# Strassen's scheme for the MLP's first product on half of the tiles, in a two-layer linear-attention and MLP kernel

## The chip, the cores and the metric

The kernel runs on one core of a Trainium2 chip. The metric is the device time of the whole program in microseconds. Of the core's engines, TensorE (PE) does matrix products into PSUM; VectorE (DVE), ScalarE (ACT) and GpSimd (POOL) do the work on elements; SyncE (SP) issues nearly all DMA transfers. Each engine works through its instructions in program order and waits on semaphores of the others.

## The reference

```python
def _A_ref(x, wqkv, wo):                 # D = 448, H = 16, Dh = 28
    qkv = (x @ wqkv) ...                 # q, k, v by heads
    phi = lambda t: jnp.where(t > 0, t + 1, jnp.exp(t)) + 1e-6
    pq, pk = phi(q), phi(k)
    kv = einsum("bhsd,bhse->bhde", pk, v); z = einsum("bhsd->bhd", pk)
    o = einsum("bhqd,bhde->bhqe", pq, kv) / (einsum("bhqd,bhd->bhq", pq, z)[..., None] + 1e-6)
    return o (heads joined) @ wo
def _B_ref(x, w1, b1, w2, b2):           # F = 1792
    return gelu(x @ w1 + b1) @ w2 + b2
x = A_x                                  # 1 x 2048 x 448
x = x + _A_ref(_layernorm(x), A_wqkv, A_wo)
x = x + _B_ref(_layernorm(x), B_w1, B_b1, B_w2, B_b2)
...                                      # the same two lines once more, same weights
```

All arrays are float32.

## The kernel before

The 2048 rows of x are 16 tiles of 128 rows, in four blocks of four tiles. F is 14 chunks of 128. Each operand of a product is split into a high part (rounded to the type float32r) and a low part (the rest, float32r too), and a product takes three matmuls: high by high, high by low, low by high. The inner size 448 is three pieces of 128 rows and one of 64; in that last piece the weights' high and low parts lie under each other in one tile of 128 rows, so that it takes two matmuls. A product over 448 is eleven matmuls.

A layer has four stages. The first (`phase1`) goes over the 16 tiles: normalize, transpose, project k and q, and gather the sums `G` over all tiles. The second (the list `ORDER`) makes the matrices that give the attention output and treats block 0. The third is the MLP, block by block: for chunk i, `mlp1(l, b, i + 1)` makes the next chunk's hp (128 features by 512 rows, eleven matmuls of 512 columns), ACT takes the gelu into g and casts it to gh, DVE makes gl; then `mlp2(l, b, i)` adds the chunk's product with w2 to four PSUM tiles y (four row tiles, three matmuls of 448 columns each). Between the two, `behind` issues the work for the following blocks by the lists PLAN_0, PLAN_1 and PLAN: `z` multiplies on POOL, `p` scales the stored q by its denominators and transposes it on DVE, `sq`/`lq` store it to DRAM and load it back spread over partitions (4 DMAs), `q` splits it, `o` is the attention product (11 matmuls of 448 columns) and the residual add with its statistics, `n` normalizes and transposes, `sx`/`lx` store and load again, `x` splits the result into the block's XH and XL. Beside block 3 the next layer's first five tiles are prepared and wk, wq are split again.

The high and low parts of w1 (`w1h`, `w1l`, `w1x`) and of w2 (`w2h`, `w2l`) are made once, in layer 0, by `background`, piece by piece, and stay in SBUF for both layers. The order on every engine is the program's order; no planner changes it.

`mlp1` takes its moving rows from a block as one run of 512 columns:

```python
def moving(self, x, c):
    return x[:, c * 512:(c + 1) * 512]
```

In the prediction, y names the products of mlp2, hp those of mlp1, gh and gl the split of the gelu's result.

Of the kernel before, what the change touches and what calls it, by code (L numbers as in the profile page):

```python
# [22 lines left out]
def linear_attn_mlp_kernel(  # L23
# [22 lines left out]
    NG = D // G  # L46
    TL = D - 64
# [115 lines left out]
    one = t512("e", 3, "one")[:, :128]  # L163
# [9 lines left out]
    none = consts.tile([128, 6], F32, name="none")  # L173
    none, rs0, sums = none[:, :1], none[:, 1:2], none[:, 2:]
    waste = t512("xn", 2, "waste")
# [3 lines left out]
    mhalf = consts.tile([128, 2], F32, name="mhalf")  # L179
    mhalf, eps = mhalf[:, :1], mhalf[:, 1:]  # L180
    pool.memset(mhalf, -0.5)
    pool.memset(eps, 1e-5)
    tiny = consts.tile([128, 1], F32, name="tiny")
    pool.memset(tiny, 1e-6)
    zc = consts.tile([128, 1], F32, name="zc")
# [11 lines left out]
    w1h = wts.tile([128, 3, F], F32R, name="w1h")  # L197
    w1l = wts.tile([128, 3, F], F32R, name="w1l")
    w1x = wts.tile([128, F], F32R, name="w1x")
    w2h = wts.tile([128, NF, D], F32R, name="w2h")  # L200
    w2l = wts.tile([128, NF, D], F32R, name="w2l")

# [22 lines left out]
    def ln_norm(stats, name, centre=OP.subtract):  # L225
        xs, mv, rs = stats
        xn = t512("xn", 2, name)
        dve.tensor_scalar(xn[:, :D], xs, mv[:, 0:1], rs, op0=centre, op1=OP.mult)
        return xn

    class Block:
        def __init__(self, key):
            at = APART if key[0] == "a" else 0
            self.rows = key[0] == "m"
            self.hi = work.tile([128, 2048], F32R, name="XH", tag="XH", bufs=2)
            self.lo = work.tile([128, 2112], F32R, name="XL", tag="XL", bufs=2)[:, at:at + 2048]

        def pieces(self, t):  # L240

            if self.rows:
                return tuple(x.rearrange("p (c t n) -> p t c n", c=4, t=4)[:, t] for x in (self.hi, self.lo))
            s = slice(t * 512, (t + 1) * 512)
            return self.hi[:, s], self.lo[:, s]

        def moving(self, x, c):

            return x[:, c * 512:(c + 1) * 512]

        def still(self, x, t, c):

            return x[:, (t * 4 + c) * 128:(t * 4 + c + 1) * 128]
# [63 lines left out]
    def spread(key, h, queues=(sp,)):  # L317
        d = stored.pop((key, h))
        r = spreads[key, h] = half("sp") if d.shape[1] == 1024 else half_square("sp", h)
# [17 lines left out]
    def turn_one(x, key, j):  # L337
# [4 lines left out]
                      x[:, TL:D].rearrange("p (m n) -> p m n", n=32)[:, None].to_broadcast([128, 2, 2, 32]))  # L342

# [19 lines left out]
    def proj(name, key, j, o=None, cs=range(4), at=(3, 6, 9, 11)):  # L363
# [3 lines left out]
        if len(cs) == 4:  # L367
            w = [wkq[name, c] for c in range(3)]
            his = [(b.still(b.hi, j, c), p) for c in range(3) for p in w[c]] + [(b.still(b.hi, j, 3), wkq[name, 3])]
            los = [(b.still(b.lo, j, c), w[c][0]) for c in range(3)] + [(b.still(b.lo, j, 3), wkq[name, 3])]  # L370
# [3 lines left out]
        for c in cs:  # L374
            if c < 3:
                hi, lo = wkq[name, c]
                pe.matmul(o, b.still(b.hi, j, c), hi, start=(c == 0), stop=False)
                pe.matmul(o, b.still(b.hi, j, c), lo, start=False, stop=False)
                pe.matmul(o, b.still(b.lo, j, c), hi, start=False, stop=False)
            else:  # L380
                pe.matmul(o, b.still(b.hi, j, 3), wkq[name, 3], start=False, stop=False)
                pe.matmul(o, b.still(b.lo, j, 3), wkq[name, 3], start=False, stop=True)
        return o

    def phi(o, name, into=None, tag="e"):

        e = t512(tag, 3 if tag == "e" else 2, name)[:, :D]
# [7 lines left out]
    def bg_pieces():  # L395
        n = 0
        both = []

        def stage():
            nonlocal n  # L400
            n += 1
            if n <= LATE:
                k = (n - 1) // 2
                if k % 2 == 0 or k > 5:
# [858 lines left out]
```

## Time and profile before

| | |
|---|---|
| time, median of 3 runs (lowest, highest) | 864.05 us (863.78, 864.33) |
| the profiled execution's own time | 864.72 us |
| its span, from first to last instruction | 863.0 us |
| PE, DVE, ACT, POOL busy | 99%, 57%, 41%, 25% of the span |
| matmuls | 4155 |
| DMA | 97.89 MB in 68681 packets |

In the rows below, a group has the line, the engine, the operation, what it writes and reads, its shape and count, then busy time, mean duration in ns, and the engine's idle time before it with what ended it. A row of one line's durations has minimum, median and maximum in ns. A row of a wait has who waited for whom, the microseconds in total, the times, and the longest. A row of the timeline has the start, the duration, and the instruction; a row of the chain has the start, the length, and the work. A matmul's duration there is longer than the distance to the next matmul's start, since matmuls are pipelined.

### The profile page before, as it was taken

The page shows a single profiled execution, that of the slowest core. Times are in us where ns is not written, and L with a number is a line of the kernel's source. Part 1 is how long each engine was busy: PE and PEld are TensorE (multiplying, and loading weights), DVE is VectorE, ACT ScalarE, POOL GpSimd, SP SyncE. Part 2 cuts the span into 40 slices and gives each one's busy share as a digit, 9 for nine tenths or more (in the row PEclk, how much of TensorE's full clock was granted, in tenths as well). Part 3 has the DMA queues.
Part 4 walks back from the last instruction along what each step waited for, and adds up shares of the span by engine and source line. Part 5 has one row for each costly group of instructions (what it writes and reads, how often), then busy time and mean ns, then how long its engine had stood idle before and what let it go on. Part 6 is the DMA issues. An engine that isn't in the chain of part 4 may idle for free.

```text
span 863.0 us, 11715 instructions
## 1 busy us (share of the span) xinstructions
PE 857.2 (99%) x4155; PEld 768.1 (89%) x4155; DVE 493.0 (57%) x962; ACT 352.8 (41%) x635; POOL 211.6 (25%) x244
## 2 busy tenths in 40 slices
PE   9999999999999999999999999999999999999998
PEld 8999988888888888888899998988888888888887
DVE  7888586559456443236477876764664383533112
ACT  7676655323323322333356565633232233233231
POOL 3576612235013012012222343120310140140000
PEclk9999999999999999999999999999999999999999
DMA  5485647633313402051146442462332423111001
GB/s 171 150 270 180 206 108 217 191 113 121 123 61 123 140 0 98 1 182 49 49 150 188 164 130 96 146 204 81 123 113 78 140 74 111 49 49 43 1 1 43
DMA packets 68681, 97.89 MB, mean 113 GB/s; under 512 B 9488, under 2 KB 62864, under 8 KB 68624
## 3 DMA queue, kind: packets, MB, share of 16 engines
q1 hardware_dynamic: 67872, 96.76, 35.0%
q8 instruction: 32, 0.52, 0.3%
q10 hardware_dynamic: 752, 0.41, 0.2%
q14 instruction: 25, 0.20, 0.1%
HBM read 57.74 MB, written 36.18 MB: 109 GB/s over the span
## 4 chain that ended last, share of the span: by engine, by line
PE 90%; DVE 4%; DMA 3%; issue 1%; ACT 1%; POOL 1%; SPq 0%; DVEq 0%; ACTq 0%; POOLq 0%
PE hp L1011 32%; PE y L1041 10%; PE y L1040 10%; PE y L1042 10%; PE psq L372 5%; PE G L658 5%; PE psk L372 5%; PE op L949 2%; PE op L948 2%; PE op L950 2%; DMA sp<-sq_a 1%; PE op L938 1%; PE op L937 1%; PE op L939 1%; PE kvp L824 1%
## 5 line engine op out<-in xcount | busy, mean ns | idle before, releaser
L1017 DVE TENSOR_TENSOR gl<-g,gh 128x512 fp32r<-128x512 f32 x112 | 83.2, 743 | 293.0 <-ACT gh L1016 293.0
L1013 ACT ACTIVATE g<-hp,b1s 128x512 f32<-128x512 f32 x112 | 77.1, 689 | 400.8 <-PE hp L1011 400.8
L1041 PE MATMUL y<-w2l,gh 128*128 128x448 f32 x447 | 163.6, 366 | 0.0
L1040 PE MATMUL y<-w2h,gh 128*128 128x448 f32 x447 | 162.0, 362 | 0.0
L1042 PE MATMUL y<-w2h,gl 128*128 128x448 f32 x447 | 160.0, 358 | 0.0
L1011 PE MATMUL hp<-XH,w1h 128*128 128x512 f32 x336 | 130.7, 389 | 0.0
L1011 PE MATMUL hp<-XH,w1l 128*128 128x512 f32 x336 | 130.7, 389 | 0.0
L1011 PE MATMUL hp<-XL,w1h 128*128 128x512 f32 x336 | 130.1, 389 | 0.0
L216 POOL TENSOR_TENSOR brs<-bve,mhalf 128x1 f32<-128x1 f32 x55 | 34.2, 622 | 258.5 <-DVE bve L215 250.8
L1040 PEld LDWEIGHTS y<-w2h,gh 128*128 128x128 f32 x447 | 83.7, 187 | 9.4
L1041 PEld LDWEIGHTS y<-w2l,gh 128*128 128x128 f32 x447 | 83.9, 188 | 7.0
L1042 PEld LDWEIGHTS y<-w2h,gl 128*128 128x128 f32 x447 | 84.0, 188 | 5.0
L1011 PEld LDWEIGHTS hp<-XL,w1h 128*128 128x128 f32 x336 | 63.1, 188 | 13.1
L1011 PEld LDWEIGHTS hp<-XH,w1h 128*128 128x128 f32 x336 | 63.0, 187 | 10.7
L1011 PEld LDWEIGHTS hp<-XH,w1l 128*128 128x128 f32 x336 | 63.1, 188 | 9.9
L1016 ACT CAST gh<-g 128x512 fp32r<-128x512 f32 x112 | 69.6, 621 | 3.6
L372 PE MATMUL psk<-wk,XH 128*128 128x448 f32 x210 | 61.8, 364 | 0.0
L372 PE MATMUL psq<-wq,XH 128*128 128x448 f32 x196 | 57.0, 365 | 0.0
L497 POOL TENSOR_TENSOR xnl<-x,xnh 128x384 fp32r<-128x384 f32 x32 | 35.0, 1094 | 73.5 <-ACT xnh L496 60.3
L355 DVE TENSOR_TENSOR XL<-sp,XH 128x512 fp32r<-128x512 f32 x58 | 47.2, 825 | 5.7 <-ACT XH L354 5.7
L883 POOL TENSOR_TENSOR pz<-pq,zb 128x448 f32<-128x448 f32 x24 | 28.2, 1174 | 89.9 <-DVE dn L894 61.8
L658 PE MATMUL G<-kh,xnh 128*128 128x448 f32 x128 | 46.7, 367 | 0.0
(194 smaller groups left out, 1500.2 us busy)
## 6 DMA issues: line engine op xcount, KB each, us to landing
x<-in_A_x_dram SPq DMA_DIRECT2D x32, 224.0 KB, 3.9
pq_d<-eq SPq DMA_DIRECT2D x32, 224.0 KB, 2.5
pq<-pq_d SPq DMA_DIRECT2D x32, 224.0 KB, 3.6
x<-x_d SPq DMA_DIRECT2D x32, 224.0 KB, 3.9
sq_a<-sq SPq DMA_DIRECT2D x13, 512.0 KB, 2.9
sp<-sq_a SPq DMA_DIRECT2D x52, 128.0 KB, 2.9
sq_q<-sq SPq DMA_DIRECT2D x12, 512.0 KB, 2.6
sp<-sq_q SPq DMA_DIRECT2D x48, 128.0 KB, 2.8
```

Source lines behind the costliest of these rows:

```text
L216: pool.tensor_tensor(rs, ve, mhalf, op=OP.pow)
L355: eng.tensor_tensor(lo.rearrange("p c (i n) -> p c i n", n=32), x, f(h), op=OP.subtract)
L372: pe.matmul(o, x, p, start=(i == 0), stop=(i == 10))
L497: pool.tensor_tensor(lo[:, :TL], xn[:, :TL], f(h[:, :TL]), op=OP.subtract)
L658: pe.matmul(acc[c], w, k, start=first and c not in others[0], stop=last and c not in others[1])
L1011: pe.matmul(hp, w, r, start=(k == 0), stop=(k == len(made) - 1))
L1013: act.activation(g, hp, AF.Gelu_apprx_tanh, bias=b1s[:, i:i + 1])
L1016: act.copy(gh, g)
L1017: dve.tensor_sub(gl, g, f(gh))
L1040: pe.matmul(acc[j], gh[:, s], w2h[:, i], start=first, stop=False)
L1041: pe.matmul(acc[j], gh[:, s], w2l[:, i], start=False, stop=False)
L1042: pe.matmul(acc[j], gl[:, s], w2h[:, i], start=False, stop=stop)
```

## The change

Blocks 0 and 1 of a layer keep the products described above (`classic`). Blocks 2 and 3, the last eight tiles, are treated together. Their 1024 rows are split into two halves of 512 columns, the inner size 448 into an upper 256 and a lower 192, and each pair of w1's chunks into its two chunks. On these two by two pieces runs Strassen's scheme (Winograd's form): seven products in place of eight, on sums and differences of the weights' pieces and of the tokens' pieces.

Each pair of chunks comes from DRAM again whenever it is used, for each layer and three times in a layer (blocks 0, 1 and the pairs of blocks 2 and 3), and is split anew into one of two buffers W1: by `chunks` for the classic blocks, by `sevens` for Strassen's pieces. `make(n)` issues one step of such a generator, and the calls of `make` are placed among the other work.

The attention work for blocks 1, 2 and 3 now all lies beside the two classic blocks, in one new list PLAN of 28 steps. The residual rows of these blocks are stored to r_d after the attention add and come back by `back` when they are needed. The token sums S1 to S4 are made in the last steps of PLAN (tokens `s` and `t`), the odd halves on DVE and the even ones on POOL, each then split into high (ACT) and low (DVE). The y products of the last two chunks of block 1 are held back into the first pair.

In a pair, block 2's two chunks go on to mlp2 beside the following products; block 3's gelu results are stored to g_d, and when all seven pairs are done `rest` loads them, splits them, and runs mlp2 for block 3 without other products, with the next layer's first tiles beside it.

The tokens' buffers XH and XL are now one tile each, with every tile's four pieces together, so that a classic product's moving rows are four runs of 128 columns:

```diff
-        def moving(self, x, c):
-            return x[:, c * 512:(c + 1) * 512]
+        def moving(self, k, c):
+            at = self.key[2] * 2048
+            return (XH, XL)[k][:, at:at + 2048].rearrange("p (t n) -> p t n", t=4)[:, :, c * 128:(c + 1) * 128]
...
-    w1h = wts.tile([128, 3, F], F32R, name="w1h")
-    w1l = wts.tile([128, 3, F], F32R, name="w1l")
-    w1x = wts.tile([128, F], F32R, name="w1x")
+    W1 = wts.tile([128, 2, 25 * 128], F32R, name="W1")
...
+    def top(x, hi, lo):
+        act.copy(hi, x)
+        pool.tensor_tensor(lo, x, f(hi), op=OP.subtract)
+    def low(x, w):
+        act.copy(w[:, :512], x)
+        pool.tensor_tensor(w[64:, 256:512], x[64:, 256:], f(w[64:, 256:512]), op=OP.subtract)
+        pool.tensor_tensor(w[:, 512:768], x[:, :256], f(w[:, :256]), op=OP.subtract)
...
+    def sevens(n):
+        came = raw(n)
+        yield
+        ...
+        low(down, w)
+        yield
+        top(t1, u[:, 6:10:2], u[:, 7:10:2])
+        dve.tensor_copy(down[:, 256:], f(w[:, 256:512]))
+        yield
+        pool.tensor_tensor(t1, t3, t1, op=OP.subtract)
+        pool.tensor_tensor(t3, t2, t3, op=OP.subtract)
+        yield
+        pool.tensor_tensor(t2, t2, t1, op=OP.subtract)
+        pool.tensor_tensor(t4, t4, t2, op=OP.subtract)
+        yield
+        act.copy(w[:, 1280:1792], up)
+        sp.dma_start(fold[:64], t4[64:, 1])
+        sp.dma_start(fold[64:], t4[:64, 1])
+        yield
+        dve.tensor_tensor(w[:, 2304:2816], up, f(w[:, 1280:1792]), op=OP.subtract)
+        yield
+        pool.tensor_tensor(t4[:, 1], t4[:, 1], fold, op=OP.add)
+        yield
+        act.copy(w[:, 1792:2304], down)
+        yield
+        dve.tensor_tensor(w[:, 2816:3072], down[:, :256], f(w[:, 1792:2048]), op=OP.subtract)
+        dve.tensor_tensor(u[:, 24], t2[:, 1], f(u[:, 16]), op=OP.subtract)
+        dve.tensor_tensor(u[64:, 17], t4[64:, 1], f(u[64:, 17]), op=OP.subtract)
+        yield
...
+    SUMS = {"S1": ("A21", "A22", OP.add), "S2": ("S1", "A11", OP.subtract),
+            "S3": ("A11", "A21", OP.subtract), "S4": ("A12", "S2", OP.subtract)}
+    def token_sum(l, name, h):
+        eng = (pool, dve)[h]
+        ...
+    def token_piece(l, name, h, eng=dve):
+        x = view(l, name, h)
+        hi, lo = (cols(placed(l, k, name, h)) for k in range(2))
+        act.copy(hi, x)
+        eng.tensor_tensor(lo, x, f(hi), op=OP.subtract)
+    PRODUCTS = {1: ((6, 7, 8, 9), "A11"), 2: ((1, 5, 3), "A12"), 3: ((0, 4, 2), "S4"), 4: ((15, 23, 17), "A22"),
+                5: ((11, 19, 13, 21), "S1"), 6: ((14, 22, 16, 24), "S2"), 7: ((10, 18, 12, 20), "S3")}
...
+    PLAN = (
+        "p10 z11",
+        ...
+        "q13 o12 n11 sx10 p20 z21",
+        ...
+        "q22 o21 n20 p30 z31",
+        "q23 o22 n21 sx20 p31 z32 sq30",
+        ...
+        "n33 lx30 sx31 tA110 b13",
+        "lx31 sS10 tA120",
+        "tS10 sS30 sS20",
+        "tS20 sS40 sS11 tS11 sS31",
+        "tS40 sS21 tS21 sS41",
+        "tA220 tA221 tS41",
     )
...
+    def eight(l, k):                     # one pair of chunks on blocks 2 and 3
+        n = first_pair(l, 2) + k
+        c = Pair(l, k, n)
+        def step():
+            if k < NP - 1:
+                make(n + 1)
+        c.product(1)
+        s1 = c.keep(c.X, "s1")           # ACT copy out of PSUM
+        if k == 0:
+            make(n, 2)
+            beside(l, k)                 # here: the pieces S30, S31
+        step()
+        if k == 0:
+            mlp2(l, 1, NF - 2)
+            c.product(2)
+            mlp2(l, 1, NF - 1)
+        c.product(5)
+        s5 = c.keep(c.Y, "s5")
+        step()
+        if k == 0:
+            dve.tensor_tensor(s1, s1, c.Z, op=OP.add)
+        if k:
+            mlp2(l, 2, 2 * k - 1)
+        c.product(6)
+        s2 = c.keep(c.X, "s2")
+        step()
+        if k == 0:
+            c.high(s1, 0)                # gelu in two halves, cast to gh
+        else:
+            c.product(2)
+            dve.tensor_tensor(s1, s1, c.Z, op=OP.add)
+            c.high(s1, 0)
+            step()
+        c.product(7)
+        dve.tensor_tensor(s5, c.X, s5, op=OP.add)
+        c.low(0)                         # gl
+        c.later(s5, 1)                   # gelu, store to g_d
+        step()
+        c.product(3)
+        dve.tensor_tensor(s2, s2, c.Y, op=OP.add)
+        c.high(s2, 1)
+        step()
+        c.product(4)
+        if k == NP - 1:
+            gb.load(l, 2)
+        c.low(1)
+        c.later(c.X, 0)
+        step()
+        if k < NP - 2:
+            make(n + 2)
+        if k:
+            beside(l, k)                 # wk, wq loads and splits, residuals back
+        step()
+        mlp2(l, 2, 2 * k)
+        step()
...
-        mlp1(l, 0, 0)
-        trans_chunks(tr)
-        for b in range(NB):
-            ...
+        for b in range(2):
+            classic(l, b, tr)
+        for k in range(NP):
+            eight(l, k)
+        if l + 1 < LAYERS:
+            table(AF.Exp)
+        rest(l)
```

Products 1, 6, 7 and 4 add up in one PSUM tile X, products 5 and 3 in Y, product 2 is Z; s1, s5 and s2 are copies of what X and Y hold at their time.

513 lines of the change are left out of this document (330 added, 183 removed), and 8 rows, old and new, of tables (ORDER, STEPS).

## The prediction

> **What bounds the kernel now.** I read the page's busy shares and slices first, then the chain of work that ended last, then TensorE's own waits.
>
> ```profile
> span 863.0 us, 11715 instructions
> PE 857.2 (99%) x4155; PEld 768.1 (89%) x4155; DVE 493.0 (57%) x962; ACT 352.8 (41%) x635; POOL 211.6 (25%) x244
> DVE  7888586559456443236477876764664383533112
> PEclk9999999999999999999999999999999999999999
> PE 90%; DVE 4%; DMA 3%; issue 1%; ACT 1%; POOL 1%; SPq 0%; DVEq 0%; ACTq 0%; POOLq 0%
> PE hp L1011 32%; PE y L1041 10%; PE y L1040 10%; PE y L1042 10%; PE psq L372 5%; PE G L658 5%; PE psk L372 5%; PE op L949 2%; PE op L948 2%; PE op L950 2%; DMA sp<-sq_a 1%; PE op L938 1%; PE op L937 1%; PE op L939 1%; PE kvp L824 1%
> ...
> PE warm L170 <- DVE one L164: 1.1, 1, 1.1
> PE psk L586 <- ACT wk L137: 0.9, 1, 0.9
> PE psk L372 <- DVE XL L355: 0.2, 1, 0.2
> ```
>
> TensorE (PE) is busy for 857.2 of 863.0 us at full clock, and its waits come to 2.2 us, nearly all at the start. Time goes down only by issuing fewer matmuls, and goes up by every new hole in PE. A busy PE need not run at its pitch, so I checked the pitch in the chain's order of time and in one timeline:
>
> ```profile
> 363.80 2.49 PE hp L1011 x11
> 368.70 2.49 PE hp L1011 x11
> ...
> 476.76 2.20 PE psq L372 x11
> ...
> 380.59 0.39 PE L1011 MATMUL hp<-XL,w1x 128*128 128x512 f32 x1
> 380.81 0.36 PE L1040 MATMUL y<-w2h,gh 128*128 128x448 f32 x1
> 381.01 0.69 ACT L1013 ACTIVATE g<-hp,b1s 128x512 f32<-128x512 f32 x1 [3.55 <-PE hp L1011]
> 381.73 0.62 ACT L1016 CAST gh<-g 128x512 fp32r<-128x512 f32 x1
> 382.39 0.70 DVE L1017 TENSOR_TENSOR gl<-g,gh 128x512 fp32r<-128x512 f32 x1 [4.20 <-ACT gh L1016]
> 383.21 0.39 PE L1011 MATMUL hp<-XH,w1h 128*128 128x512 f32 x1
> 383.44 0.39 PE L1011 MATMUL hp<-XH,w1l 128*128 128x512 f32 x1
> ...
> ```
>
> Eleven matmuls of 448 columns take 2.20 us, 0.2002 each. One chunk of the MLP is 368.70 − 363.80 = 4.90 us and holds eleven of 512 and twelve of 448; 4.895 − 12 × 0.2002 = 2.49, so a 512-column matmul costs 0.2265 us of PE. The same rows give the way round: 0.20 us after the next product begins ACT starts on the old one, and gl is there 2.3 us after PE ended hp.
>
> **The product counts.** A pair of chunks on two blocks takes 2 × 2 × 11 = 44 matmuls of 512 columns; Strassen's seven products take 6+5+5+5+6+6+6 = 39 (the list PRODUCTS: four weight pieces give six matmuls, three give five, since the 64 last rows carry high and low part in one piece). Seven pairs, two layers: 14 × 5 = 70 fewer, 70 × 0.2265 = 15.9 us. Nothing else in PE's list changes number. This is the whole gain, and the ceiling: 864.05 − 15.9 = 848.2.
>
> **The two classic blocks.** All attention output work of blocks 1 to 3 now lies beside two blocks instead of three.
>
> ```profile
> 134.00:202.00 68.00, 68.00 (x322) 60.17 (x321) 42.77 (x79) 25.68 (x44) 24.71 (x22) 1.00 0.55 169
> 202.00:264.00 62.00, 62.00 (x295) 55.13 (x295) 34.21 (x69) 17.88 (x29) 9.12 (x9) 1.00 0.33 110
> 264.00:333.00 69.00, 69.00 (x329) 61.32 (x328) 36.95 (x73) 20.98 (x34) 15.60 (x14) 1.00 0.23 78
> ...
> L1017 DVE TENSOR_TENSOR gl<-g,gh 128x512 fp32r<-128x512 f32 x112 | 83.2, 743 | 293.0 <-ACT gh L1016 293.0
> L355 DVE TENSOR_TENSOR XL<-sp,XH 128x512 fp32r<-128x512 f32 x58 | 47.2, 825 | 5.7 <-ACT XH L354 5.7
> L431 POOL TENSOR_TENSOR w2l<-stg,w2h 128x448 fp32r<-128x448 f32 x14 | 16.5, 1181 | 36.2 <-ACT w2h L430 36.2
> ...
> L1045 DVE TENSOR_TENSOR x<-y,x x32: 610/614/625, 213.6 to 858.8; 128x448 f32<-128x448 f32 x32
> ```
>
> The columns after the stretch are its length, then PE, weight loads, DVE, ACT, POOL. DVE: 42.8 + 34.2 + 37.0 = 113.9 us. Out go 14 gl (10.4), 4 adds of y (2.5) and 8 block pieces (6.6); in come 14 token pieces at 0.825 and four half sums of some 0.75 (14.6): 109 us in 28 × 4.895 + 12 × 2.20 = 163.5 us, 67%. Per tile the parts q, o, n, p come to (113.9 − 42 × 0.743 − 12 × 0.614 − 12 × 0.825) / 12 = 5.5 us; the densest steps hold all four (of four tiles) and a gl, 6.2 us of DVE in 4.9 + 2.2 = 7.1 us of PE; gl has 4.9 − 2.3 = 2.6 us to spare, so I cost this at nothing. The cover is that slack; should backlog pass it, PE waits for gl once per step. POOL gets the w1 splits, four instructions per pair at about 0.84 (between the rows for 64 and 384 columns below): 14 × 3.4 = 47 us on top of 49.4 less some 14 of w2 (12 of the 14 in its row), half its time. ACT gets 1.4 us per pair (two casts of 256, one of 512). SP gets two loads of w1 per pair, twelve stores and loads of r_d, twelve issues each, and is past its work two steps ahead; all of it waits behind spreads whose store must land first, as before. Layer 0 loses its w1 splits in the first phase and has two pairs' splits beside the Q products; PE has no hole there to win (0.2 us). Zero for these.
>
> The moving rows of the classic product now come as four runs of 128 columns. No row shows such a read by PE. Every product of before has one run; I take zero, as the data per column are the same, and price the other end below.
>
> **The pairs in steady order.** A pair is 39 × 0.2265 + 24 × 0.2002 = 13.64 us of PE: product 1 to 1.36, 5 to 2.72, y to 5.12, 6 to 6.48, 2 to 7.61, 7 to 8.97, 3 to 10.1, 4 to 11.24, y to 13.64. Three places wait: product 7 for the copy s2 on ACT (0.20 + 0.62 after 6, product 2 gives 1.13), product 4 for the add into s5 on DVE (0.20 + 0.69, product 3 gives 1.13), and y for gh and gl (s1 at 8.5, two half gelus and cast to 10.0, gl at 10.8 behind s5; needed at 11.24 and 11.6). All hidden by 0.2 to 0.8 us. ACT is packed from 7.8 to 14 and free again for the next s1 at 15.2. The weight chain of the next pair (about 5.7 us of POOL, 2 of ACT, 2 of DVE) has its late link in the two fold transfers.
>
> ```profile
> wq<-Mh SPq DMA_DIRECT2D x2, 56.0 KB, 2.8
> ...
> wq<-Mh SPq DMA_DIRECT2D x2, 28.0 KB, 4.5
> ```
>
> They are issued behind the store of g, near 10.5 to 11.5; landing after 2.8 or 4.5 us, POOL's add, ACT's cast and DVE's three low pieces end at 16 to 17.5, and product 6 of the next pair wants them at 18.8. Zero, with 1.3 us left at the bad end.
>
> **The join, twice.** Here the cover runs out. Call T the end of the last classic product (chunk 13 of block 1). PE has 1.36 (product 1), 2.40 (y, chunk 12), 1.13 (2), 2.40 (y, chunk 13), then 5, 6, 7 with 1.36 each and 3 with 1.13: product 4 is due at T + 12.5. It needs DVE's add into s5. DVE is free from gl of chunk 12, at T − 4.9 + 2.3 = T − 2.6, and has in order nine pieces, four half sums, gl of chunk 13, W1's low parts (one of 512, one of 256, two of 128: 1.65), two copies of 256 (0.5, an estimate under the 0.42 of the row for 256), four adds of y, s1 and s5.
>
> ```profile
> L355 DVE TENSOR_TENSOR XL<-sp,XH x58: 677/684/1640, 46.1 to 783.2; 128x512 fp32r<-128x512 f32 x58
> L1017 DVE TENSOR_TENSOR gl<-g,gh x112: 681/693/1478, 138.1 to 856.0; 128x512 fp32r<-128x512 f32 x112
> L905 DVE SCALAR_TENSOR_TENSOR pq<-pq,rd x32: 615/1181/1374, 105.5 to 708.2; 128x448 f32<-128x448 f32 x32
> 147.08 1.16 POOL L883 TENSOR_TENSOR pz<-pq,zb 128x448 f32<-128x448 f32 x1
> 147.47 1.25 DVE L905 SCALAR_TENSOR_TENSOR pq<-pq,rd 128x448 f32<-128x448 f32 x1
> L292 DVE TENSOR_TENSOR XL<-tp,XH 128x256 fp32r<-128x256 f32 x4 | 1.6, 422 | 0.4 <-ACT XH L290 0.2
> L290 ACT CAST XH<-tp 128x256 fp32r<-128x256 f32 x4 | 1.4, 368 | 0.1
> L978 POOL TENSOR_TENSOR x<-x,b2b 128x448 f32<-128x448 f32 x32 | 41.9, 1329 | 0.0
> L497 POOL TENSOR_TENSOR xnl<-x,xnh 128x384 fp32r<-128x384 f32 x32 | 35.0, 1094 | 73.5 <-ACT xnh L496 60.3 <-PE psk L372 13.1
> L498 POOL TENSOR_TENSOR xnh<-x,xnh 128x64 fp32r<-128x64 f32 x32 | 14.5, 452 | 0.0
> ...
> ```
>
> At the medians (minimum, median, maximum in these rows): 9 × 0.684 + 5 × 0.69 + 1.65 + 0.5 + 4 × 0.614 + 2 × 0.69 = 15.6 us, so T + 13.0: at least 0.6 us late even if DVE never waits. It does wait: the S1 and S2 halves go sum on DVE, cast on ACT, low part on DVE, 0.65 us empty each, 1.3. And it meets POOL, which in the same time has the S4 half (about 1.45) and four weight differences (0.84 each), 4.8 us. DVE operations with two SBUF inputs stretch beside POOL: the row of pq went from 0.615 to 1.25 us under POOL's pz, while the adds from PSUM stay at 610 to 625 ns. Low end: none, 0.6 in all. High end: POOL's 4.8 us fully in DVE's way, 6.7. I take the row nearest: pieces average 0.825 against 0.684, 0.14 each with POOL busy a quarter of these stretches; at four times that share 0.56 each, five such operations, 2.8, a third of it inside the empty 1.3. So 0.6 + 1.3 + 1.9 = 3.8 us a layer, 7.6 in all. It shows first at product 6 (third of W1's low parts on DVE), then at 7 (S3) and at 4.
>
> The Trainium skill has a rule on this, in "SBUF — State Buffer", section "Who interferes with whom": a VectorE operation with two SBUF inputs and a GpSimd operation that reads SBUF exclude each other, and the second blocks until the first ends. The pq row's 1.25 us agrees. By it alone the join costs its high end, which is the second rival.
>
> **After the pairs.** Block 3's second product runs alone, 2.40 us a chunk, against 0.62 + 0.69 of ACT and DVE for its split.
>
> ```profile
> L205 ACT ACT_TABLE_LOAD x4 | 5.1, 1283 | 1.3 <-PEq L1249 1.3
> ...
> 367.00:432.00 65.00, 65.00 (x308) 57.39 (x307) 31.07 (x55) 23.67 (x40) 13.27 (x13) 1.00 0.28 93
> ```
>
> In layer 0 this table load puts the first gh late and DVE's low part ahead of three adds of y: 0.7 us. The next layer's first tiles lay beside block 3 before (the stretch from 367 us, 31.1 us of DVE with 13 gl and the splits of wk and wq in it); without those splits, which move to the pairs, they fit into 14 × 2.40 = 33.6 us with one chunk of slack for gl: zero.
>
> **The sum.** Against the profiled execution's own 864.72 us: − 15.86 + 7.6 + 0.7 = 857.2; the median of the runs lies 0.67 lower: 856.5.
>
> **The rivals.**
> 1. The join is hidden, as DVE gets ahead and POOL is done before it: 0 to 2 us a layer, 848.9 to 852.9. For it: the four POOL differences depend on nothing of PE and may be through early. Against: 15.6 us of DVE in 15.1 of PE.
> 2. The lock is complete: 6.7 a layer and the same 0.7, 862.3 (861 to 864.5). For it: 1181 as the median of pq. Against: gl's median is the undisturbed 693.
> 3. The strided moving rows cost PE. Two layers have 2 × 28 × 11 = 616 such matmuls. From 0.2265 and 0.2002 a matmul's fixed part is 0.0265 for 64 columns, hence 0.2265 − 0.212 = 0.0145; three more starts each, 0.0435 × 616 = 26.8 us: 883, slower. It decides from 8 / 616 = 13 ns a matmul. For it: the two sides of a split are never seen in the trace. Against: nothing in the chain depends on how rows lie.
> 4. The fold chain is late in every pair by over 0.6 us: 14 × 0.6 eats what is left. Against: 1.3 us of slack at the bad end.
>
> **Chances.** Forecast (852.9 to 861): 0.57. Rival 1: 0.16. Rival 2: 0.15, and it lies across the bound, 0.06 of it faster, 0.08 the same, 0.01 slower. Rival 3: 0.07. Rival 4 and unseen holes: 0.05, 0.01 of it the same. Faster by over 0.2% (1.7 us, about what a measurement of this kernel can tell from no change) 0.79, same 0.09, slower 0.12. Range 850 to 863: it leaves out a third of rival 1, rivals 3 and 4 and the end of 2.
>
> **What would show it.** 1162 matmuls of 512 columns in the MLP's first product at 0.2265 pitch; the classic ones at the same pitch (rival 3 otherwise). PE's waits with DVE low parts and s5 as releasers at two places of the span, some 3 to 4 us each, each just behind the second classic block, and none in pairs 1 to 6. DVE pieces near 1.2 us there. If PE waits for gl in the classic blocks, my zero there is wrong; if for W1 in later pairs, the chain's.

## The result, and the profile after

The changed kernel takes 930.15 us (929.2 to 931.75 in four runs) where the kernel before, measured beside it, took 864.19: a ratio of 1.0765, 95% interval 1.0746 to 1.0783. It is 66 us slower than before, and 82 us above the 848.2 that the matmul counts promised. One execution of e1_raw_early (1724.71 us) and one of e8_before_off64 (1070.89 us), far slower than the others of their kernels, are left out of the times below. The first fence is from the page of the kernel after: span, busy time, the granted clock in forty slices, the chain that ended last by engine and by line.

```profile
span 927.9 us, 12697 instructions
PE 878.6 (95%) x4085; PEld 760.6 (82%) x4085; DVE 590.8 (64%) x1094; ACT 444.0 (48%) x869; POOL 390.8 (42%) x460
PEclk9999999998999999999999999999999999999999
PE 49%; DMA 18%; DVE 12%; ACT 6%; SPq 5%; issue 4%; POOL 4%; DVEq 0%; ACTq 0%; POOLq 0%
DMA raw<-in_B_w_dram 8%; PE G L726 8%; PE psk L385 7%; PE psq L385 7%; PE hp L1201 5%; PE y L1233 3%; PE y L1231 3%; PE y L1232 3%; DMA temp<-in_B_w_dram 3%; DMA sq_q<-sq 3%; PE hx L1143 2%; SPq L333 2%; DVE gl L1178 2%; ACT g L1155 2%; DVE pq L975 1%
```

The 70 matmuls are gone (4155 to 4085). But PE carries 49% of the chain instead of 90%, and DMA 18% instead of 3%: its first entry is the load of w1 for the pairs (`raw<-in_B_w_dram`, 8% of the span), with the classic blocks' load (`temp`) and the stores of sq_q behind it. PE's waits, the largest ones (line, what it waited for: us in all, times, longest; hx, hy and hz are a pair's tiles X, Y and Z, op is the attention product, ql and qh the split of its q, W the pieces of w1):

```profile
PE hx L1143 <- ACT s L1147: 20.4, 12, 2.7
PE op L1025 <- DVE ql L368: 4.2, 4, 1.6
PE y L1233 <- DVE gl L1178: 4.2, 4, 1.2
PE hx L1143 <- DVE W L478: 2.6, 2, 1.3
PE hp L1201 <- POOL W L434: 2.3, 4, 1.1
PE hy L1143 <- DVE W L472: 2.1, 2, 1.2
```

The stretches of layer 0 (length, then busy PE, weight loads, DVE, ACT, POOL, the granted clock, DMA share, GB/s): classic blocks, join, six steady pairs, and the rest up to the next layer.

```profile
134.99:306.23 171.24, 166.76 (x754) 142.99 (x752) 115.70 (x214) 64.77 (x119) 80.45 (x86) 0.98 0.62 190
306.23:327.99 21.76, 17.43 (x64) 12.43 (x63) 19.19 (x27) 10.94 (x22) 12.53 (x14) 0.92 0.13 47
327.99:424.47 96.48, 86.39 (x379) 71.62 (x378) 40.06 (x65) 52.51 (x110) 42.71 (x49) 0.98 0.30 93
424.47:470.01 45.54, 41.44 (x193) 35.43 (x192) 29.63 (x55) 17.36 (x32) 16.70 (x18) 1.00 0.70 227
```

From these lengths I take what the matmuls would need at the pitches of before (the pitch is the time from one matmul's start to the next one's): 158.65 us for the classic blocks (28 × 2.4915 + 26 × 2.4024 + 12 × 2.2022), 13.63 for the join, 6 × 13.64 for the pairs and 16 × 2.40 for the rest. What is left is the loss of a stage. The table has it for layer 0 / layer 1, worked out in this way from the trace of each kernel:

| us lost in | classic | join | six pairs | rest | time of the kernel |
|---|---|---|---|---|---|
| after | 12.6 / 11.1 | 8.1 / 8.2 | 14.6 / 15.1 | 7.1 / 1.7 | 930.15 |
| first load early (e1b) | 10.8 / 12.4 | 7.3 / 7.7 | 1.5 / 1.5 | 5.8 / 1.9 | 898.67 |
| no classic loads (e2) | 4.6 / 4.3 | 6.1 / 6.6 | 15.3 / 11.4 | 7.1 / 1.7 | 906.7 |
| split load (e16) | 8.0 / 6.3 | 6.1 / 7.1 | 2.1 / 1.4 | 2.3 / 1.4 | 886.66 |
| split load and four more edits (e17) | 4.1 / 2.7 | 4.6 / 4.6 | 1.5 / 1.4 | 2.7 / 1.3 | 871.66 |

For the kernel after the eight losses sum to 78.5; with some 2 us in the first stages that is 848.2 + 80.5 = 928.7, against 930.15. Every stage lost, those that I had costed at nothing most.

This is how the pairs lose, in the timeline of pair 1 of layer 0 (start, length, and in brackets the idle time before):

```profile
332.20 0.58 SPq L423 DMA_DIRECT2D raw<-in_B_w_dram  x1
339.25 0.62 ACT L432 CAST W<-raw 128x512 fp32r<-128x512 f32 x1 [6.14 <-DMA raw<-in_B_w_dram]
340.55 0.59 ACT L1147 COPY s<-hx 128x512 f32<-128x512 f32 x1
341.19 1.65 PE L1143 MATMUL hx<-S,W 128*128 128x512 f32 x6 [2.73 <-ACT s L1147]
```

SP issues the second part of pair 2's load at 332.20. Within pair 1, ACT comes to the cast that starts pair 2's weight chain, and stands 6.14 us until the load is there. The copy s2 (at 340.55), whose data PE had finished, is behind that cast in ACT's order; product 7 needs s2's bank, and PE stands 2.73 us. The wait is booked to ACT, but a DMA ends last. That the load takes 6.5 us, the same timeline shows; why, the windows behind its issue show in the DMA share:

```profile
332.20:334.00 1.80, 1.80 (x10) 1.53 (x9) 0.92 (x3) 0.90 (x2) 0.00 (x0) 1.00 0.94 240
334.00:336.00 2.00, 2.00 (x11) 1.85 (x10) 0.00 (x0) 0.00 (x0) 0.00 (x0) 1.00 0.38 111
336.00:338.00 2.00, 2.00 (x10) 1.66 (x9) 0.00 (x0) 0.00 (x0) 0.00 (x0) 1.00 0.14 49
338.00:339.00 1.00, 0.47 (x3) 0.03 (x1) 0.00 (x0) 0.00 (x0) 0.00 (x0) 1.00 0.07 26
```

From 336 on the share is 0.14 at 49 GB/s: two of sixteen engines work, 2 / 16 = 0.125, and 128 KB / 49 GB/s is 2.7 us. That is the copy of w1's last 64 rows into both halves of the tile, one transfer with an outermost dimension of 2 (`to_broadcast([2, 64, 256])`). The Trainium skill says just this in "DMA: Bandwidth & Descriptors", section "Rules for kernel authors": a transfer whose outermost dimension is below 16, such as a zero-stride broadcast of c copies, is confined to at most c engines. The trace agrees (0.14). I had not applied it.

### The profile page after: what moved, and what is told of

It reads as the page before. It is cut to its first block, busy times and chain, and to the rows that moved or that the text cites. A ratio compares the mean times of both kernels' runs of the same rounds, so it can differ in the third digit from the quotient of the medians.

```text
span 927.9 us, 12697 instructions
## 1 busy us (share of the span) xinstructions
PE 878.6 (95%) x4085; PEld 760.6 (82%) x4085; DVE 590.8 (64%) x1094; ACT 444.0 (48%) x869; POOL 390.8 (42%) x460
## 4 chain that ended last, share of the span: by engine, by line
PE 49%; DMA 18%; DVE 12%; ACT 6%; SPq 5%; issue 4%; POOL 4%; DVEq 0%; ACTq 0%; POOLq 0%
DMA raw<-in_B_w_dram 8%; PE G L726 8%; PE psk L385 7%; PE psq L385 7%; PE hp L1201 5%; PE y L1233 3%; PE y L1231 3%; PE y L1232 3%; DMA temp<-in_B_w_dram 3%; DMA sq_q<-sq 3%; PE hx L1143 2%; SPq L333 2%; DVE gl L1178 2%; ACT g L1155 2%; DVE pq L975 1%
## 5 line engine op out<-in xcount | busy, mean ns | idle before, releaser
L1201 PE MATMUL hp<-XH,W 128*128 128x512 f32 x392 | 126.5, 396 | 2.3 <-POOL W L434 2.3
L1203 ACT ACTIVATE g<-hp,b1s 128x512 f32<-128x512 f32 x56 | 38.4, 686 | 145.1 <-PE hp L1201 145.1
L1231 PEld LDWEIGHTS y<-w2h,gh 128*128 128x128 f32 x447 | 84.5, 189 | 14.6 <-ACT gh L1174 3.8
L1201 PEld LDWEIGHTS hp<-XH,W 128*128 128x128 f32 x392 | 73.8, 188 | 18.2 <-POOL W L434 4.0
L213 POOL TENSOR_TENSOR brs<-bve,few 128x1 f32<-128x1 f32 x55 | 35.9, 652 | 122.7 <-DVE bve L212 119.1
L1201 PE MATMUL hp<-XL,W 128*128 128x512 f32 x224 | 86.2, 393 | 0.0
L428 POOL TENSOR_TENSOR W<-temp,W 128x256 fp32r<-128x256 f32 x56 | 48.3, 882 | 76.8 <-ACT W L427 65.0
L1143 PE MATMUL hx<-S,W 128*128 128x512 f32 x168 | 49.5, 432 | 23.4 <-ACT s L1147 20.4
L1143 PEld LDWEIGHTS hx<-S,W 128*128 128x128 f32 x168 | 32.8, 202 | 36.1 <-ACT s L1147 25.6
L1155 ACT ACTIVATE g<-s,b1s 128x256 f32<-128x256 f32 x84 | 38.2, 502 | 25.2 <-DVE s L1407 8.6
L1201 PEld LDWEIGHTS hp<-XL,W 128*128 128x128 f32 x224 | 42.1, 188 | 9.6
```

The costliest lines, as they stand in the source:

```text
L428: pool.tensor_tensor(lo, x, f(hi), op=OP.subtract)
L1143: pe.matmul(o, w, r, start=(k in (1, 5, 2) and i == 0), stop=(i == len(made) - 1), skip_group_check=True)
L1155: act.activation(g[:, s].rearrange("p (u i n) -> p i u n", u=2, i=4), x[:, s].rearrange("p (i u n) -> p i u n", u=2, i=4), AF.Gelu_apprx_t ...
L1201: pe.matmul(hp, w, r, start=(k == 0), stop=(k == len(made) - 1))
L1203: act.activation(g, hp, AF.Gelu_apprx_tanh, bias=b1s[:, i:i + 1])
L1231: pe.matmul(acc[j], gh[:, s], hi, start=first, stop=False)
```

## The experiments

**The late load of the steady pairs.** e1_raw_early issues the load of pair k + 2 behind product 1 of pair k instead of behind its product 4; e1b_raw_early is the same kernel again, for its profile.

```diff
             make(n, 2)
             beside(l, k)
+        if k < NP - 2:
+            make(n + 2)
         step()
...
-        if k < NP - 2:
-            make(n + 2)
         if k:
```

> The changed kernel with one move: the load of w1 for the pair after next is issued behind the first product of a pair instead of at its end, some 11 us earlier. Theory L (late loads): in each pair ACT stands some 5 to 6 us before the cast that needs the load (landing 6.5 to 7 us after its issue, the cast due 4 us after it), and product 7 waits for ACT's copy s2 behind it. Then the six pairs lose their 15 us per layer but for 1 to 3 us, the waits of hx for s (20.4 us) nearly vanish, and the time falls by 22 to 28 us, to 902 to 908. Rival W (work): ACT and DVE have more to do in a pair than PE's 13.6 us leave room for; the copy is late wherever the load is issued, and the time stays within 5 us of 930.

> The kernel with the early load for the pairs once more, for its trace: the waits of hx for ACT's copies at 1 to 4 us in all instead of 20.4, the pairs within 3 us of their pitch in each layer, and the classic blocks as slow as before (11 to 12.6 us over).

Measured: ratio 1.0407 (1.039 to 1.0425), 899 us, 31 less than after and more than the 22 to 28 expected; e1b 898.67. The pairs lose 1.5 us instead of 15 and no wait for s is left in them: the standing cast was nearly the pairs' whole loss.

**Three suspects taken out singly and together.** e2_classic_noload leaves out the loads of w1 in the classic blocks from the third pair on (old weights are split instead). e4_join_nopool leaves out GpSimd's four weight differences of the first pair on eight tiles. e5_three_out has both and the early load.

```diff
+        if kind == "c" and n - first_pair(l, 0) >= 2:
+            return x                              # e2, e5
...
+        if ahead[n][2]:                           # e4, e5
             pool.tensor_tensor(t1, t3, t1, op=OP.subtract)
...
```

> The changed kernel with the w1 loads of the classic blocks left out but for the first two of a layer (the same raw tile is split again, so the MLP's weights are wrong there); the splits on ACT and POOL stay. The two classic blocks lose 12.6 and 11.1 us against their pitch. Theory L: these 12 loads of 512 KB per layer stand in the DMA queue before the stores and spreads of q and m (stores landing after 7.3 us instead of 2.6) and late themselves; without them the classic blocks lose 4 to 6 us each, and the time falls by 10 to 16 us. Rival D (density): three blocks' attention work in two blocks is too much for DVE and its chains of stores and loads; without the w1 loads the time falls by less than 5 us.

> The changed kernel without the four differences of weight pieces on POOL for the first pair of each layer (its products are wrong). From the last classic product to the first y of block 2 PE takes 21.8 us instead of 13.6, twice. Theory K (lock): DVE's operations there last 1.2 to 1.3 us instead of 0.68 since POOL's differences hold them up, some four times 0.5 to 0.6 us; without them the join shrinks by 2 to 3 us a layer, the time by 4 to 6. Rival L: the join is late because ACT waited 4.6 us for the first pair's load ahead of the gelu of chunk 12, and DVE follows; then it shrinks by less than 1 us a layer.

> The three earlier edits together: the early load for the pairs, no w1 loads in the classic blocks but two per layer, and no weight differences on POOL for the first pair (the last two leave work out). If the three causes are separate, their gains add: 30 + 23 + 13 us off 930 gives 864, and PE's waits fall under 12 us. If they are one cause seen three times (ACT behind loads, PE's clock lowered after each hole), the gains overlap, and the time stays at 872 to 885.

Measured: e2 906.71 (ratio 1.0491, 1.047 to 1.0513); e4 916.68 (1.0606, 1.0588 to 1.0624); e5 879.59 (1.0178, 1.0161 to 1.0195). Without loads the classic blocks lose 4.5 us instead of 12 and the join 2 less, since its first load is in time. e4 takes 2.3 and 2.7 us off the join; the rest of its 13 lies in stages that it doesn't touch, and the repeat below (e14) shows that two measurements of one kernel can lie 8 us apart. Early load, e2 and e4 bring 31, 23 and 13 us singly and 51 together, so their gains overlap. In e5 the join still loses 4.5: in layer 0 PE waits there for VectorE (W's low parts 1.25 us, the add into s5 1.51) and for ACT's copy s2 (0.68).

**The strided rows** (rival 3 of the prediction), made in the kernel before: XH and XL in the layout of after, read as four runs of 128 columns.

```diff
-            return x[:, c * 512:(c + 1) * 512]
+            return x.rearrange("p (t c n) -> p c t n", t=4, c=4)[:, c]
...
```

> The kernel before, with the tokens' pieces of an MLP block lying tile by tile as in the changed kernel, so that each of its 1232 products of 512 columns reads four runs of 128 columns. The changed kernel's classic products stand 0.232 us apart instead of 0.2265. Theory S (the strided read costs the 5.5 ns): 1232 x 0.0055 = 6.8 us, 870 to 872 us, and the pitch in the trace 0.232. Rival: the pitch comes from elsewhere (Strassen's products, whose rows lie in one run, also show up to 0.232), and the time stays within 1.5 us of 864.

Measured: 864.09, ratio 1.0002 (0.9993 to 1.0011). Runs of 128 columns cost nothing.

**How the loads hold up the classic blocks.** e7_prefetch has the early load and issues each classic load one chunk earlier. e6_packed adds a copy of w1 into rows of 4 KB in the first stage, so that a load is one transfer of long rows.

```diff
+            if i % 2 == 0 and not ends:
+                make(n + 1)                       # e7, e6: load one chunk earlier
...
-        sp.dma_start(x[:, :768]..., w1[:TL, ...])
-        sp.dma_start(x[:, 768:], w1[TL:, ...][None].to_broadcast([2, 64, 256]))
+        sp.dma_start(x, packed[p])                # e6
...
```

> The early load for the pairs, and the loads of the classic blocks issued one chunk earlier too, ahead of the chunk's waits for stores; nothing left out. Theory L1 (the loads come too late for the casts that wait for them): the classic blocks regain 5 to 9 us a layer, as they did without the loads (7 us), and the join 2 us, as the first pair's load is there in time; 882 to 888. Rival L2 (the loads' transfers hold up the stores and spreads in the DMA queues wherever they are issued): the classic blocks stay 10 us over their pitch, 896 to 900.

> As the run with both loads early, and w1 copied once, in the first phase of layer 0, into a DRAM array with each pair's 128 rows of 4 KB in a row, so that each load is one transfer of 128 pieces of 4 KB instead of two with 512 pieces of 1 KB. Rival L2: each load holds the queues for a shorter time (6.5 us now, 3 to 4 then); 5 to 10 us less than the run with both loads early. Theory L1: 0 to 3 us less, since early loads are there anyway.

Measured: e7 902.33 (1.0434, 1.0417 to 1.045), no better than the early load alone and above both of its ranges: the classic blocks lose 16.3 and 13.4. e6 888.06 (1.0276, 1.0261 to 1.0292), 14 us less than e7 where 5 to 10 were expected: they lose 5.4 and 5.3, though the copy costs 8.4 us in the first stage. So it isn't when the loads come but what they are. The transfers' rows, KB each and median us from issue to landing, in this order before, after and in e6 (sq_q is the stored q, sp what is loaded back spread over partitions):

```profile
sq_q<-sq SPq DMA_DIRECT2D x12, 512.0 KB, 2.6
```

```profile
sq_q<-sq SPq DMA_DIRECT2D x12, 512.0 KB, 7.3
sp<-sq_m SPq DMA_DIRECT2D x48, 128.0 KB, 6.8
r_d<-x SPq DMA_DIRECT2D x24, 224.0 KB, 6.3
```

```profile
sq_q<-sq SPq DMA_DIRECT2D x12, 512.0 KB, 3.0
sp<-sq_m SPq DMA_DIRECT2D x48, 128.0 KB, 4.2
r_d<-x SPq DMA_DIRECT2D x24, 224.0 KB, 3.0
```

Beside the loads a store took 7.3 us instead of 2.6; the spread, the split (ql, qh) and PE's attention products wait behind it, which is PE's second wait above. One such store of after, behind a load of w1 issued at 203.07 and 203.55:

```profile
207.35 0.38 SPq L321 DMA_DIRECT2D sq_q<-sq  x1
212.50:215.50 3.00, 1.66 (x4) 1.49 (x5) 2.07 (x2) 2.64 (x5) 2.27 (x3) 0.59 0.12 44
216.03 1.28 SPq L333 DMA_DIRECT2D sp<-sq_q  x3
```

From 207.5 to 212 us the DMA share is 1.04; from 212.5 it is 0.12, two of sixteen engines, and only at 216.03 the loads that need the stored rows are issued, 8.7 us behind the store. I blamed the short rows. That was wrong, as e16 shows.

**TensorE's pitch.** In stretches without any stall eleven first-product matmuls still took 2.55 us (2.49 before) and twelve second-product ones 2.45 (2.40), some 10 us in all. My first theory was that the operands start 64 bytes off a multiple of 128. e8_before_off64 moves all tiles of before by 64 bytes, e9_after_aligned moves one small tile of after.

```diff
-    none = consts.tile([128, 6], F32, name="none")
+    none = consts.tile([128, 22], F32, name="none")      # e8
...
-        dn = consts.tile([128, H], F32, name="dn", tag="dn", bufs=1)
+        dn = work.tile([128, H], F32, name="dn", tag="dn", bufs=1)      # e9
```

> The kernel before, with the small constant tile 64 bytes longer, so that every weight and operand tile behind it starts at 64 mod 128 bytes of its partition instead of 0; no instruction differs. Theory M (a TensorE operand that starts 64 bytes off a multiple of 128 lengthens each matmul): the second-product matmuls go from a pitch of 0.200 us towards the 0.204 of the kernel after, the first-product ones from 0.227 towards 0.2315; some 1,344 x 0.004 + 1,232 x 0.0045 + about 2 in the attention stages = 12 to 14 us, so 875 to 878. Rival (the longer pitch comes from the layout of XH and XL side by side, or from the mean over the records): 864 within 0.3%.

> The kernel after, with one 64-byte tile (dn) moved from the pool of constants to that of the work tiles, so that all weight and operand tiles start at a multiple of 128 bytes but the last two, which hold S1's high pieces and S3; no instruction differs. Theory M: pitches back to 0.200 and 0.227 except in the products that read those two tiles, 9 to 13 us less than 930.2, so 917 to 921; the stalls stay as they are. Rival: 930 within 0.3%.

Measured: e8 864.65, ratio 1.0 (0.9991 to 1.001). e9 916.58 (1.0602, 1.0586 to 1.0619), but with the pitches unchanged, 2.55 and 2.45. The theory falls. What is left is where the tiles lie to each other: before, the tiles of weights and of moving rows start alike modulo 256 bytes; after, W1 and the activations start 128 bytes off w2, XH and XL. The matmuls G, whose operands are alike in both, keep their 2.21. e12_before_rel128 makes that difference in before, for the first product alone; e13_after_rel takes it out of after (both get room from unused bytes of attention tiles); e14_after_again is after once more, beside them.

```diff
-    w1x = wts.tile([128, F], F32R, name="w1x")
+    w1x = wts.tile([128, F + 32], F32R, name="w1x")             # e12
...
-    XL = wts.tile([128, NX * 512 + APART], F32R, name="XL")
+    XL = wts.tile([128, NX * 512 + APART + 32], F32R, name="XL")      # e13, e15, e17
...
```

> The kernel before with 128 bytes of padding behind w1x, so that XH, XL, w2 and all tiles behind them start at 128 mod 256 bytes while w1h, w1l and w1x stay at 0; w2h and gh shift together and stay alike. (Four attention tiles lose 128 unused bytes each to make room.) Theory R (a TensorE matmul is slower where its moving rows and its weights start 128 bytes apart modulo 256): the eleven first-product matmuls of a chunk take 2.55 us instead of 2.49, as in the kernel after, the twelve second-product ones stay at 2.40; 112 chunks x 0.06 = 6.7 us, so 870 to 872. Rival: 864.6 within 0.3%, both at 2.49 and 2.40.

> The kernel after with 128 bytes of padding between XL and W1, so that W1, the activations and the work tiles start at the same place modulo 256 bytes as w2, XH and XL. Theory R: 11 first-product matmuls in 2.49 us instead of 2.55, twelve second-product ones in 2.40 instead of 2.45, and the attention's products with XH back to 0.200; about 10 us less than the repeat of the kernel after in the same call (8 to 13). Rival: no difference to the repeat.

> The kernel after once more, on this chip, as the yardstick for the two runs beside it and for the aligned kernel, which took 916.6 with the same instructions and the same TensorE pitches. If the 64 bytes saved the 14 us, this is 930 within 0.4%. If the kernel's stalls differ between chips (its granted clock was 0.986, that of the aligned kernel 0.996), this is anywhere from 912 to 930.

Measured: e12 873.68 (1.0112, 1.0091 to 1.0133), e13 918.18 (1.0631, 1.0603 to 1.0659), e14 922.33 (1.0673, 1.0656 to 1.0691). The chain in order of time shows the eleven matmuls of a chunk in after, e12 and e13:

```profile
170.74 2.55 PE hp L1201 x11
```

```profile
268.73 2.57 PE hp L1011 x11
273.70 2.57 PE hp L1011 x11
```

```profile
260.40 2.49 PE hp L1201 x11
267.52 2.49 PE hp L1201 x11
```

128 bytes of padding lengthen the first product of the kernel before by 0.08 us a chunk; 112 × 0.08 = 9.0 us, and the run is 9.6 longer (6.7 were expected, from 2.55), while its twelve second-product matmuls stay at 2.40. The same 128 bytes bring 2.49 and 2.40 to the kernel after. There only 4 us of the 8 to 13 expected came of it. In e13's trace layer 0's classic blocks lose 11.4 us, in e14's 8.5, so waits took some of the gain; why they are longer stays open.

**All together, with packed rows.** e10_all: early load, earlier classic loads, e9's tile, and each w1 tile stored as long rows during the first classic block. e11_all_join: at the join S3's second half goes to GpSimd, and the four additions of y behind that of s5. e15_packed_join_rel: e6 with the join's changes and the padding.

```diff
+            packed[n] = dram([128, 1024], F32, f"w1p{n}")
+            sp.dma_start(packed[n], x)            # e10, e11, in layer 0's first block
...
-                token_piece(l, tok[:-1], int(tok[-1]))
+                token_piece(l, tok[:-1], int(tok[-1]), (dve, pool)[int(tok[-1])])      # e11, e15, e17
...
```

> The kernel after with the first load of each pair issued before its first product, the loads of the classic blocks one chunk earlier, aligned tiles as in the run above, and each w1 tile stored once, during the first classic block of layer 0, as rows of 4 KB that all later loads read in one transfer. The packed kernel took 888.1, of which 8.4 us was the copy in the first stage, which here lies in the first classic block (cost there 5 to 12 us against packed, since that block keeps the slow loads, 16 against 5). Under M another 10 to 13 less: 866 to 876. Without M: 878 to 888.

> As the run above, and at the join the subtraction of S3's second half on GpSimd instead of VectorE, and the four additions of y of the second block behind VectorE's addition of s5. If VectorE's queue sets the join (it is busy there from 313.5 to 325.1 us of the packed profile, and TensorE waits 0.8, 1.2, 0.7 and 1.5 us for it), 2 to 5 us less than the run above over both layers. Rival (GpSimd and VectorE share a port, so the moved piece costs as much as it saves): 0 to 2 less.

> All that helped together: first load of a pair before its first product, the classic blocks' loads one chunk earlier, w1 packed once into rows of 4 KB in the first stage (888.1 with these three), S3's second half on GpSimd and the y additions behind s5 at the join (1.4 us less before), and the padding between XL and W1. Theory R and separate gains: 888.1 - 1.4 to 3.5 - 10 = 875 to 877. If stalls take the place of the shorter matmuls: 880 to 886.

Measured: e10 894.7 (1.0343, 1.0325 to 1.0362), above its range: the old loads and the stores share layer 0's classic blocks, which lose 18.3. e11 893.33 (1.0337, 1.032 to 1.0355): its join loses 4.4 us instead of 6.1, 3.5 over both layers, but only 1.4 of it arrives. e15 880.43 (1.0184, 1.0166 to 1.0202), 8 less than e6 and at the edge of "stalls take the place".

**The transfer with the outer 2.** e16_after_split changes this one transfer in the kernel after. e17_split_all adds the early load, the earlier classic loads, the padding and the join's changes, without a packed copy.

```diff
-        sp.dma_start(x[:, 768:], w1[TL:, ...][None].to_broadcast([2, 64, 256]))
+        for h in range(2):
+            sp.dma_start(x[h * 64:(h + 1) * 64, 768:], w1[TL:, ...])
```

> The kernel after with one edit: the load of w1's last 64 rows into both halves of the tile, one transfer whose outermost dimension is 2, becomes two transfers of 64 partitions. Theory T (the transfer with the outer 2 runs on two of the 16 DMA engines: behind a pair's raw load the trace shows a DMA share of 0.14 at 48 GB/s for 2.7 us, and 128 KB / 48 GB/s = 2.7 us; stores and spreads that use all engines end only when those two come free): raw lands some 2.5 us earlier, so the pairs lose 2 to 8 us a layer instead of 13 to 15, the stores sq_q land after 3 to 5 us instead of 7.3 and the classic blocks lose 5 to 8 instead of 12; 25 to 45 us less than 930 or 922, so 880 to 900. Rival (the load is late because 384 rows of 1 KB are slow, or because SP issues it late): 915 to 930, and SP's one more issue per load, 0.6 us, shows.

> The split load, the first load of a pair before its first product, the classic blocks' loads one chunk earlier, the padding between XL and W1, and the join's two changes; no packed copy of w1. Under T the copy isn't needed: 848.2 plus 12 for the join, 3 to 8 for each layer's classic blocks, 2 to 4 after the pairs, 2 for the pairs: 868 to 880. Rival (the rows of 1 KB cost by themselves): the classic blocks stay at 9 to 13 a layer, 882 to 892.

Measured: e16 886.66 (1.0265, 1.0248 to 1.0283), 43 us less than after and 36 less than its repeat. e17 871.66 (1.0091, 1.0076 to 1.0106). The transfers of e16:

```profile
sq_q<-sq SPq DMA_DIRECT2D x12, 512.0 KB, 3.1
sp<-sq_m SPq DMA_DIRECT2D x48, 128.0 KB, 3.4
r_d<-x SPq DMA_DIRECT2D x24, 224.0 KB, 2.0
raw<-in_B_w_dram SPq DMA_DIRECT2D x28, 64.0 KB, 3.6
```

The stores are back at 3.1 us, though every row is as short as in after. The stretch from 212.5 us above fits: while the broadcast held two engines, the store's last rows waited for these two. The pairs lose 2 us without any earlier load. So one transfer carried 36 to 43 of the 82 us, and the early load and the packing had only gone around it.

What remains in e17 is 871.66 − 848.2 = 23.5; its stages lose 22.9, of it 9.2 in the two joins, with PE's waits and clock as follows (its page, then its waits):

```profile
span 869.1 us, 12747 instructions
PE 851.5 (98%) x4085; PEld 753.0 (87%) x4085; DVE 587.0 (68%) x1092; ACT 441.8 (51%) x869; POOL 390.2 (45%) x462
PEclk9999999999999999999999999999999999999999
```

```profile
PE hx L1144 <- DVE W L479: 2.5, 2, 1.2
PE y L1234 <- DVE gl L1179: 2.4, 3, 0.9
PE hy L1144 <- DVE W L473: 1.8, 2, 0.9
```

No variant of the changed kernel beats the kernel before; the best is 0.9% behind it.

## Why the prediction was wrong, step by step

- **The product counts** hold: 4155 − 4085 = 70 matmuls fewer. The price per matmul, 0.2265, did not: 2.55 / 11 = 0.232 in the classic blocks. I asked what the strides of the rows cost (nothing, e3) and not where the tiles lie. Tiles 128 bytes apart modulo 256 cost 9.6 us in the kernel before (e12) and, by their pitches, some 10 in the kernel after (e13).
- **The steady pairs at zero** is the step that failed worst: 14.6 and 15.1 us. I named the right place, product 7 waiting for the copy s2 with 1.13 us of cover, and priced the fold transfers as the weight chain's late link. The chain's first link, the load, I didn't price at all, nor that ACT's cast stands in line ahead of s2. e1 shows the order, e16 why the load was late.
- **The classic blocks at zero** failed by 12.6 and 11.1 us. Engine time was counted well: DVE 115.7 us against my 109. The loads were counted as two issues on SP's queue, not as transfers that hold engines which the stores need (2.6 to 7.3 us). Some 3 us of each loss is the longer pitch (28 × 0.06 + 26 × 0.05); without the loads 4.6 and 4.3 are left (e2).
- **The join at 3.8 a layer** (0.6 for DVE's queue, 1.3 for its waits, 1.9 for POOL) named the right queue and was too small: 8.1 and 8.2, above even the 6.7 of rival 2. It put the late load at nothing, and the queue and its waits too low. In layer 0 ACT stands 4.59 us for the pair's first load ahead of the gelu of chunk 12, so its gl starts at 304.77, 1.5 us before T = 306.23, not at T − 2.6:

```profile
302.88 0.62 ACT L432 CAST W<-raw 128x512 fp32r<-128x512 f32 x1 [4.59 <-DMA raw<-in_B_w_dram]
304.77 0.96 DVE L1178 TENSOR_TENSOR gl<-g,gh 128x512 fp32r<-128x512 f32 x1 [4.39 <-ACT gh L1174]
308.10 1.23 DVE L1108 TENSOR_TENSOR S<-sp 128x512 f32<-128x512 f32 x1
308.86 1.07 POOL L463 TENSOR_TENSOR raw<-raw 128x256 f32<-128x256 f32 x1
313.57 0.68 DVE L1108 TENSOR_TENSOR sp<-S,sp 128x512 f32<-128x512 f32 x1
```

  Beside POOL's differences a DVE sum (L1108) takes 1.23 us, alone 0.68, as rival 2's lock would make it for operations that overlap. Taken out, the differences give 2.5 us a layer (e4; I had 1.9) and the late load 2 (e2, e7; I had nothing). The 4.5 left in e5, where neither is there, stands against the 0.6 + 1.3 that I had for DVE's queue and its waits. The 0.6 itself is 0.5 by the numbers beside it (T + 13.0 against T + 12.5). PE waited at the y of chunk 13 and at products 5, 6 and 7, in layer 1 at 4 too; I had named 6, 7 and 4.
- **After the pairs, 0.7**: 7.1 and 1.7. Layer 0's gh waited 3.92 and 5.05 us for gb (block 3's gelu results, loaded back), a load that I had not priced. With the split load 2.3 and 1.4 remain.
- **The rivals.** Rival 3 falls (e3; its price took 0.0265 for 0.2265 − 0.2002 = 0.0263, which changes nothing), rival 1 was never near, rival 4 named the pair's chain but the wrong link. My last sentence on what would show an error ("If PE waits for gl in the classic blocks ..., if for W1 in later pairs") missed both forms: PE waited for ql and for an ACT copy. All four rivals dealt with engines or with the fold; none with the 45 MB of new traffic (97.9 to 142.9 MB), of which 42 loads of w1, 512 KB each, are 22 MB; one transfer in each of these loads carried about half of the loss.

## What to carry to other kernels

Price every new transfer like a new instruction: which engines it uses, how long it holds them, who lands behind it. A low DMA share while something waits for a DMA (0.14 here) can mean that the transfer uses few engines; look at its outermost dimension. And when an in-order engine is handed the first consumer of a load, list what stands behind that instruction, for that is who will wait.

## What the runs showed of the hardware

**Where tiles lie changes the matmul's time**: eleven matmuls take 2.49 us when the tiles of weights and moving rows start alike modulo 256 bytes, 2.55 to 2.57 when they start 128 apart (e12, e13; other distances were not measured); a common shift of 64 changes nothing (e8, 864.65 us against 864.64). The Trainium skill, "TensorE: Matmul & The Clock Gate", section "Step-by-step: what each phase is for", says that weights and moving rows have ports of their own and loading the one takes nothing from the other. A lengthening of 0.08 us in 2.49 that comes and goes with the distance between the two suggests that this isn't exact; how they meet, no run here shows.

**A hole can cost more than its length.** In the kernel after the clock falls to half for 3.4 us at a time behind some of the holes (here at 213.0, in the second of two holes, 1.03 us at 210.6 and 1.56 us at 212.3); in the last stretch the attention product's matmuls start 0.37 us apart instead of 0.20:

```profile
208.00:211.80 3.80, 2.77 (x13) 1.94 (x12) 0.72 (x1) 1.75 (x4) 1.51 (x3) 1.00 1.05 298
211.80:215.20 3.40, 1.84 (x6) 1.34 (x7) 2.47 (x3) 2.34 (x5) 2.97 (x3) 0.68 0.18 62
215.20:218.60 3.40, 3.40 (x11) 3.01 (x10) 3.30 (x6) 1.04 (x3) 0.00 (x0) 0.50 0.40 113
```

The trace counts seven such stretches in after, two of them in a row, 24 us at half speed or at most 12 lost; three in its repeat e14, which is 7.8 us faster with the same instructions; two in e9; eight in e13; none ahead of the last matmul in the kernel before and in e17. Which holes trigger one changes from execution to execution. What the stretches cost in all is not shown: e13 took 918.75 us at a mean granted clock of 0.985 and 922.1 at 0.993, and e14 took 921.7 at 0.994 and 922.0 at 0.988, so the time doesn't simply follow the clock. Of the 14 us between after and e9, at most 8.5 are such stretches; the rest stays open. Two kernels with stalls are better compared side by side and by stages than by a few us between measurements made apart.
